# A gated long convolution and a token mixer: other order and other shapes for the loads of the first chunk

## The chip, the core and the metric

The kernel runs on one core of one Trainium2 chip. A core has TensorE (matrix products), VectorE, ScalarE and GpSimd (elementwise work), SyncE, which issues most of the transfers, and 16 DMA engines that carry them. The metric is the device time of one execution in microseconds (us), lower is better. The profile calls the engines PE (and PEld for its weight loads), DVE, ACT, POOL and SP; "SPq" and "ACTq" rows are DMA issues on SyncE's and ScalarE's queues.

## What is computed

One block on x = q, S = 2048 tokens by D = 640 channels, in 32-bit floats:

```python
mod = (silu(c) @ w_mod)                      # six rows of 640: sa, ca, ga, sb, cb, gb
h = layernorm(q) * (1 + ca) + sa
kv = short_conv(k, shift_k) * v              # 4 taps, causal, per channel
y = long_conv(kv, ssm_k) + kv * ssm_D        # causal, over all 2048 tokens, by FFT
x = q + ga * (h * y)
h = layernorm(x) * (1 + cb) + sb
out = x + gb * mlp_over_tokens(h)            # 2048 -> 1728 -> 2048, GELU, biases
```

## The kernel before

**Stages.** The first stage is the gated long convolution, in five chunks of 128 channels (loop at line 503); the second is the token mixer (from line 648). The convolution of a chunk is done by matrix products: `step1` (line 208, products of line 216) makes the first transform of kv (side 0) and of ssm_k (side 1), `f2` (line 222, products of line 232) the second transform together with the product of the two spectra, `i2` (line 253, products of line 261) and `i1` (line 268, products of line 277) the inverse. `gate` multiplies the result by the modulated layer norm A1 and adds it to q.

**How tokens lie.** A token is 32 m + 16 b + j. In the tiles of q, XH, partition 64 b + m holds the 16 rows j, so each half of the partitions belongs to one b. k, v, ssm_k and the taps are loaded by halves in the same way, h = 0 and 1 for 64 channels each (lines 127 to 153). Before, q comes in sixteen DMAs (lines 485 to 488): for every even j and each b one of 64 partitions with two neighbouring rows, that is 5,120 contiguous bytes a partition.

**What sets the order.** The schedule is written out by hand: every engine runs its instructions in the order of the program, and a DMA waits on the engine that issues it until the place that it writes is free; whatever stands behind it on that queue waits too. All transfers that matter here stand on SyncE's queue; ScalarE's queue has half of the first k and v, the first taps and the first ssm_D.

**Around the first chunk.** After the kv of chunks 0 and 1 (VectorE, with a share on GpSimd), SyncE issues the taps of chunk 2 (line 476), q, and the first four of five pieces of w_mod (line 494): piece kk is 128 rows of w_mod by the 1,920 columns of the first three modulation rows, one DMA each, cut into 2,560-byte runs. Piece 0 lies where ssm_k is loaded (T_aux), pieces 2 and 3 where the constant V1 of the inverse transform will lie (T_v1), piece 4 in P, which the spectra use until the end of f2.

Then, in chunk 0: VectorE takes the statistics of q (lines 526 to 529); TensorE does `step1(0, t)` for chunk 1, transposes the staged vectors (b1, b2 and c, in T_g), does i2(0), four of the five products with w_mod (`mod_part`, line 347), i2(1), the fifth product, the three rows that are spread over the partitions (`mod_row`, line 358), i1 for both halves, each followed by `gate`, and `step1(1, t)`, with which chunk 1 can start. SyncE issues ssm_k of chunk 1 when the first product has read piece 0 (`load_ks(1)`, line 546), V1 when the fourth has read piece 3 (line 547), and then k and v of chunk 2. ScalarE normalizes q (line 284) in sixteen operations of 128 x 128, in four portions; VectorE then applies the modulation rows (`po`).

Of the kernel before, what the change touches and what calls it, by code (L numbers as in the profile page):

```python
# [15 lines left out]
DC = 128  # L16
# [33 lines left out]
def mixer_kernel(ctx: ExitStack, tc: tile.TileContext, q, k, v, shift_k, ssm_k, ssm_D, w1, b1, w2, b2, c,  # L50
# [23 lines left out]
    def dram(t, offset, ap):  # L74
        return bass.AP(tensor=t.tensor, offset=t.offset + offset, ap=ap)
# [66 lines left out]
                           dram(k, 29 * D + DC * c + 64 * h, [[32 * D, 63], [D, 3], [1, 64]]))  # L142

    def load_taps(c, eng=sync):
        for h in range(2):
            eng.dma_start(TR[64 * h:64 * h + 64], dram(shift_k, (DC * c + 64 * h) * 4, [[0, 64], [1, 256]]))

    def load_ks(c, eng=sync):
        for h in range(2):
# [58 lines left out]
    def step1(side, t, later=False):  # L208

        ps = psum()  # L210
        for a in range(8):
            i = 8 * t + a
            lhs = KSP[:, i] if side else X.rearrange("p (m i) -> p i m", i=32)[:, i]
            o = 512 * (a % 2) + 128 * (a // 2)
            for ri in range(2):
                pe.matmul(ps[64 * ri:64 * ri + 64, o:o + 128], lhs, F1[:, 128 * ri:128 * ri + 128], start=True,  # L216
                          stop=True)
        evac = lambda: act.activation(Z[:, side, t].rearrange("p a k e -> p e a k"),  # L218
                                      ps.rearrange("p (e a k) -> p e a k", a=8, e=2), AF.Copy)
        return evac if later else evac()  # L220
# [60 lines left out]
    def a1_ops(c):  # L281

        g = lambda G: G[:, None, c * DC:(c + 1) * DC].to_broadcast([128, 16, DC])
        ac = [lambda j=j: act.activation(A1[:, j], XR(j, DC * c, DC), AF.Identity, scale=rs1[:, j:j + 1],
                                         bias=nm1[:, j:j + 1]) for j in range(16)]
        po = [lambda: TT(dve, A1, A1, g(G1), ALU.mult), lambda: TT(dve, A1, A1, g(G0), ALU.add)]
        if c == 0:
            def scaled(h):
                a, gh = A1[:, 8 * h:8 * h + 8], lambda G: G[:, None, 0:DC].to_broadcast([128, 8, DC])
                return [lambda: TT(dve, a, a, gh(G1), ALU.mult), lambda: TT(dve, a, a, gh(G0), ALU.add)]  # L290
            po = scaled(0) + scaled(1)
        return ac, po
# [46 lines left out]
    def mod_load(i, kk, place):  # L339
        sync.dma_start(place, dram(w_mod, 128 * kk * 6 * D + i * 640, [[6 * D, 128], [1, 1920]]),  # L340
                       max_dma_last_dim=2560)
# [140 lines left out]
    for t in range(4):  # L482
        step1(1, t)

    for j in range(0, 16, 2):
        for b in range(2):
            sync.dma_start(XH[j // 8][64 * b:64 * b + 64, j % 8:j % 8 + 2],
                           dram(q, (16 * b + j) * D, [[32 * D, 64], [D, 2], [1, D]]))

    three = lambda t: [t[:, 640 * j:640 * j + 640] for j in range(3)]  # L490
    pl = [three(t) for t in (T_aux, T_aux[:, 2048:3968], T_v1, T_v1[:, 1920:3840], P)]

    for kk in range(4):
        mod_load(0, kk, (T_aux[:, 0:1920], T_aux[:, 2048:3968], T_v1[:, 0:1920], T_v1[:, 1920:3840])[kk])

    fill = kv_ops(3)

# [5 lines left out]
    for c in range(NC):  # L503
        cn = c + 1 if c + 1 < NC else None
        ac, po = a1_ops(c)
        pend_m = pend_a = None
        for g in range(8):
            m_, a_ = f2(g)
            if pend_m:
                pend_m()  # L510
            if pend_a:
                pend_a()
            pend_a, pend_m = (pend_m and pa_next), m_
            pa_next = a_
            if c:
                for f_ in ac[2 * g:2 * g + 2]:
                    f_()
            dv(-(-len(fill) // max((6 if c else 8) - g, 1)))
            if c and cn is not None and g == 3:
                perm_add(cn)  # L520
        pend_m()
        if pend_a:
            pend_a()
        pa_next(dve if c else pool)
        if c == 0:
            for j in range(16):
                for h in range(2):
                    dve.bn_stats(bst[:, j, h, :], XR(j, 320 * h, 320))
                dve.bn_aggr(mv[:, j, :], bst[:, j, 0:2, :])
        if c and c + 2 < NC:  # L530
            taps()
            if c + 3 < NC:
                load_taps(c + 3)
        if c == 0:
            mod_load(0, 4, P[:, 0:1920])
            for t in range(4):
                step1(0, t)
            ps = psum()
            pe.transpose(ps[:, 0:36], stg, ID[0:36, 0:36])
            act.activation(cols, ps[:, 0:36], AF.Copy)  # L540
            act.activation(sil, cols[:, 30:35], AF.Silu)
            i2(0)
            for kk in range(4):
                mod_part(tap, kk, pl[kk])
                if kk == 0:
                    load_ks(1)
            sync.dma_start(T_v1[:, 0:4096], c_v1, max_dma_last_dim=4096)
            rstd(rs1, nm1, 0, 16)
            run(ac[0:4])
            i2(1)  # L550
            mod_part(tap, 4, pl[4])
            load_k(2, 1)
            load_k(2, 2)
            load_v(2, 2)
            load_halo(2)
            load_k(2, 0)
            load_v(2, 0)
            load_v(2, 1)
            load_k(2, 3)
            load_v(2, 3)  # L560
            mod_sum(tap, T_kt[:, 0:640])
            run(ac[4:8])
            pool.tensor_scalar(PW, TR.rearrange("p (i s) -> p s i", s=4), 1.0, None, op0=ALU.mult)
            run(kv_ops(2, pool))
            for i in range(3):
                mod_row(i, T_kt[:, 0:640])
            taps()
            load_taps(3)
            perm_add(1, dve)
            perm(1)  # L570
            load_ks(2)
            run(ac[8:16])
            run(po[0:2])
            fill.extend(kv(3, ((0,), (1, 2), (3,))))
        elif cn is not None:
            for t in range(2):
                step1(0, t)
            perm(cn)
            if c + 2 < NC:
                fill.extend(kv(c + 3 if c + 3 < NC else None))  # L580
            else:
                fill.extend(x1s(cc, j) for cc in range(c) for j in range(16))
        else:
            for kk in range(3, 5):
                mod_load(3, kk, pl[kk])
            T_wb = [mem("w0", 4096, "wb0"), mem("w1", 4096, "wb1")]
            split_w(0)
            run(po)
            for kk in range(3):
                mod_part(tap, kk, three(pl[kk]))  # L590
            load_w(1, T_aux[:, 0:2048])
            load_w(2, P)
            load_w(3, X)
        if c:
            dv(7 if cn is not None else 8)
            i2(0)
            if cn is None:
                split_w(1)
                split_w(2, mem("in", 4288, "wb2"))
            else:  # L600
                run(po)
                step1(0, 2)
            i2(1)
            if cn is not None:
                step1(0, 3)
                dv(3)
                if c + 2 == NC:
                    load_w(0)
        if cn is None:
            for kk in range(3, 5):  # L610
                mod_part(tap, kk, three(pl[kk]))
            split_w(3, mem("y", 4096, "wb3"))
            load_w(4)
            mod_sum(tap, T_t[:, 0:640])
        if c and cn is not None and c + 2 < NC:
            load_ks(c + 2)
        for half in range(2):
            ps = i1(half)
            if c and cn is None:
                dv(4)  # L620
            elif c and half:
                dv(3)
            elif c:
                k0 = step1(1, 0, True)
            elif half:
                run(po[2:4])
            if cn is not None:
                gate(c, ps, half)
            elif half == 0:
                gate(c, ps, 0, dve)  # L630
        if cn is not None:
            spill(c)
        if cn is not None:
            if c:
                k0()
            for t in range(1 if c else 0, 4):
                step1(1, t)
            if cn == NC - 1:
                dv(12)
                fill.extend(x1s(c, j) for j in range(16))  # L640
                pl = [T_in[:, 0:1920], T_in[:, 1920:3840], T_aux[:, 0:1920], T_z[:, 0:1920], T_z[:, 1920:3840]]
                for kk in range(3):
                    mod_load(3, kk, pl[kk])
            else:
                dv(11 if c else 8)
# [354 lines left out]
```

## Time and profile before

| | us |
|---|---|
| three timed runs: median | 741.24 |
| lowest, highest | 734.45, 748.2 |
| the profiled execution | 737.33 |
| its span, first to last instruction | 735.5 |
| TensorE busy in it | 653.1 |
| VectorE busy | 499.4 |
| ScalarE busy | 299.5 |
| GpSimd busy | 176.2 |

In the rows of an engine's instructions in order of time, the first number is the start in us from the span's start, the second the time taken, then engine, line, operation, tiles, shape and count; square brackets give idle time ahead of it and what ended it. A 32-bit product appears as more than one record. In rows that group instructions, the numbers behind the first bar are busy us and mean ns of one, those behind the second the idle time before them. In rows of windows each engine has busy us and number of instructions, then come the granted clock of TensorE, the mean busy share of the 16 DMA engines and the GB/s that they moved. Rows of waits have us in total, times, and the longest. The line 59 in a row is a helper through which elementwise operations are issued.

### The profile page before, as it was taken

How to read it: one execution, taken by the hardware profiler on the slowest of the kernel's cores; microseconds unless marked ns; L12 is line 12 of the kernel's file. 1: busy time of each engine (PE TensorE's matmuls, PEld its weight loads, DVE VectorE, ACT ScalarE, POOL GpSimd, SP SyncE). 2: the span in 40 equal slices, each digit the busy share in tenths (PEclk: the TensorE clock that was granted, in tenths of full speed). 3: DMA queues.
4: the chain of work that ended last, by engine and by line, in shares of the span. 5: the costliest groups of instructions: out<-in, count | busy, mean ns of one | idle time of the engine just before them, and what ended most of it. 6: DMA issues, size and time to landing. Idle time of an engine off the chain costs nothing.

```text
span 735.5 us, 20693 instructions
## 1 busy us (share of the span) xinstructions
PE 653.1 (89%) x9107; PEld 630.5 (86%) x9107; DVE 499.4 (68%) x857; ACT 299.5 (41%) x441; POOL 176.2 (24%) x176
## 2 busy tenths in 40 slices
PE   0797969999999989655899999999999989999997
PEld 0787749989989978544899999999999989999997
DVE  7756659969877548488994321231298958888886
ACT  0432465645646535425665512321235322333222
POOL 5197048626329047022440000000000000000000
PEclk9999889999999999657899999999999999999999
DMA  9989988445420174950000535335163333555410
GB/s 180 241 235 255 265 228 167 97 80 132 89 61 4 29 198 151 187 116 2 0 1 21 95 77 96 58 59 110 55 186 101 92 117 110 153 164 172 145 55 36
DMA packets 171921, 84.90 MB, mean 115 GB/s; under 512 B 88852, under 2 KB 165431, under 8 KB 171831
## 3 DMA queue, kind: packets, MB, share of 16 engines
q1 hardware_dynamic: 167282, 82.26, 45.5%
q10 hardware_dynamic: 4548, 1.31, 1.1%
q8 instruction: 71, 1.16, 0.7%
q14 instruction: 20, 0.16, 0.1%
HBM read 73.07 MB, written 10.49 MB: 114 GB/s over the span
## 4 chain that ended last, share of the span: by engine, by line
PE 58%; DVE 22%; issue 6%; DMA 4%; POOL 4%; ACT 3%; SPq 2%; ACTq 0%; DVEq 0%; POOLq 0%
PE pst L424 26%; PE pst L216 9%; PE pst L941 7%; PE pst L232 6%; DVE m_w L59 4%; PE pst L261 4%; POOL y L59 3%; PE pst L277 3%; DVE m_x L59 3%; DVE tap L59 3%; DVE kt L59 2%; ACT m_w L854 2%; PE pst L866 2%; DVE m_x L875 1%; DVE m_v L59 1%
## 5 line engine op out<-in xcount | busy, mean ns | idle before, releaser
L232 PE MATMUL pst<-z,w 128*64 128x64 f32 x2560 | 96.8, 241 | 11.7 <-ACT z L218 6.1
L232 PEld LDWEIGHTS pst<-z,w 128*64 128x64 f32 x2560 | 95.3, 142 | 13.6 <-ACT z L218 7.3
L424 PE MATMUL pst<-r_z,wb 128*128 128x320 f32 x504 | 82.9, 321 | 16.4 <-ACT r_z L685 11.3
L59 POOL TENSOR_TENSOR y<-p 128x256 f32<-128x256 f32 x72 | 90.4, 1304 | 26.8 <-DVE p L59 26.6
L424 PEld LDWEIGHTS pst<-r_z,wb 128*128 128x128 f32 x504 | 79.1, 198 | 18.3 <-ACT r_z L685 12.5
L59 DVE TENSOR_TENSOR p<-pst,kt 128x512 f32<-128x512 f32 x80 | 52.7, 690 | 28.5 <-ACT kt L236 19.3
L216 PE MATMUL pst<-v,x 128*64 128x128 f32 x640 | 46.0, 303 | 23.6 <-DVE x L59 23.6
L218 ACT ACTIVATE z<-pst 128x1024 f32<-128x1024 f32 x40 | 45.8, 1146 | 48.6 <-PE pst L216 28.4
L216 PEld LDWEIGHTS pst<-v,x 128*64 128x64 f32 x640 | 44.0, 221 | 24.2 <-POOL t L449 23.6
L424 PE MATMUL pst<-h_x,wb 128*128 128x320 f32 x336 | 51.1, 309 | 0.0
L424 PEld LDWEIGHTS pst<-h_x,wb 128*128 128x128 f32 x336 | 49.7, 188 | 0.0
L236 ACT ACTIVATE kt<-pst 128x512 f32<-128x512 f32 x40 | 25.2, 630 | 59.4 <-PE pst L232 38.8
L261 PEld LDWEIGHTS pst<-v,y 32*128 32x128 f32 x1280 | 42.6, 204 | 6.8 <-issue 2.6
L261 PE MATMUL pst<-v,y 32*128 32x64 f32 x1280 | 44.7, 291 | 4.2 <-DVE y L59 1.4
L746 ACT ACTIVATE pst<-pst,sm 128x640 f32<-128x640 f32 x14 | 10.7, 767 | 86.1 <-PE pst L424 86.1
L59 DVE TENSOR_TENSOR wb<-x,wb 128x1024 fp32r<-128x1024 f32 (+1 forms) x32 | 36.8, 1188 | 12.0 <-ACT wb L413 11.9
L866 PE MATMUL pst<-r_z,m_w 128*128 128x320 f32 x222 | 42.8, 312 | 1.9 <-DVE m_w L59 1.4
L216 PE MATMUL pst<-v,p 128*64 128x128 f32 x640 | 37.8, 274 | 2.4 <-issue 2.4
L854 ACT ACTIVATE m_w<-m_v 128x896 fp32r<-128x896 f32 x24 | 22.2, 950 | 42.4 <-DVE m_v L59 29.5
L424 PE MATMUL pst<-h_a,wb 128*128 128x320 f32 x252 | 38.8, 309 | 0.0
L424 PE MATMUL pst<-r_v,wb 128*128 128x320 f32 x252 | 38.8, 309 | 0.0
L216 PEld LDWEIGHTS pst<-v,p 128*64 128x64 f32 x640 | 35.2, 137 | 3.6 <-issue 3.2
(213 smaller groups left out, 1272.2 us busy)
## 6 DMA issues: line engine op xcount, KB each, us to landing
x<-in_B_w_dram SPq DMA_DIRECT2D x24, 512.0 KB
m_v<-in_B_w_dram SPq DMA_DIRECT2D x15, 384.0 KB
x<-in_B_w_dram SPq DMA_DIRECT2D x14, 384.0 KB
aux<-in_A_ssm_k_dram SPq DMA_DIRECT2D x10, 512.0 KB
in<-in_A_k_dram SPq DMA_DIRECT2D x36, 128.0 KB
in<-in_A_v_dram SPq DMA_DIRECT2D x36, 128.0 KB
m_x<-xs SPq DMA_DIRECT2D x28, 160.0 KB
out_dram<-m_x SPq DMA_DIRECT2D x28, 160.0 KB
```

The costliest lines, as they stand in the source:

```text
L59: TT = lambda eng, o, a, b, op: eng.tensor_tensor(o, a, b, op=op)
L216: pe.matmul(ps[64 * ri:64 * ri + 64, o:o + 128], lhs, F1[:, 128 * ri:128 * ri + 128], start=True, stop=True)
L218: evac = lambda: act.activation(Z[:, side, t].rearrange("p a k e -> p e a k"), ps.rearrange("p (e a k) -> p e a k", a=8, e=2), AF.Copy)
L232: pe.matmul(ps[64 * h:64 * h + 64, o:o + 64], W2[k1 // 32][:, 2 * (k1 % 32) + ri], rhs, start=True, stop=True)
L236: act.activation(kt.rearrange("p (m i) -> p m i", i=32), pv[:, :, 1], AF.Copy)
L261: pe.matmul(pp[qd // 2][:, o:o + 64], Y[p, ri, i:i + 2].rearrange("p i k -> p (i k)"), V2[p, 64 * ri:64 * ri + 64], start=ri == 0, stop=ri ...
L277: pe.matmul(ps[64 * b:64 * b + 64, 512 * e + 64 * jj:512 * e + 64 * jj + 64], V1[p, ri, n2], T2[p, :, 32 * ri + n2], start=ri == 0, stop=r ...
L424: pe.matmul(ps[0:m, h, 0:320], w_.bitcast(F32R), r_[:, 320 * h:320 * h + 320].bitcast(F32R), start=first and i == 0, stop=last and i == 2)
L746: act.activation(p, p, AF.Gelu_apprx_tanh, bias=B1C[:, f:f + 1])
L854: act.activation(W[n][0].bitcast(F32R), a(w_), AF.Copy)
L866: pe.matmul(bank[n], w[:, i].bitcast(F32R), r.bitcast(F32R), start=i == 0 and k == 0, stop=i == 6 and k == 2)
L941: pe.matmul(acc[s][:, h, 0:320], w[:, f_].bitcast(F32R), u[r + h].bitcast(F32R), start=f_ == 0 and k == 0, stop=f_ == NF - 1 and k == 2)
```

## The change

Everything concerns chunk 0 and the loads ahead of it.

- The taps of a chunk come in one DMA instead of two.
- ssm_k of chunk 1 is loaded ahead of q.
- q comes in sixteen DMAs of one row j each, for all 128 partitions; the source pattern is [[16 D, 2], [32 D, 64], [1, D]].
- Each piece of w_mod comes in three DMAs of 640 columns, at other places: pieces 0 and 1 in T_v1, 2 in T_aux, 3 in T_kt and T_t, 4 in G0, G1 and T_t. Three are issued behind q, two after the transpose.
- The transpose stands ahead of `step1(0, t)`, the five products behind it in a row, i2(0) and i2(1) after them. V1 is issued after the second product.
- The layer norm of q is done on VectorE in sixteen operations, ahead of the modulation rows. GpSimd's taps and its kv of chunk 2 stand behind the products in the program; ssm_k of chunk 2 is issued ahead of the taps of chunk 3.

```diff
-        for h in range(2):
-            eng.dma_start(TR[64 * h:64 * h + 64], dram(shift_k, (DC * c + 64 * h) * 4, [[0, 64], [1, 256]]))
+        eng.dma_start(TR, dram(shift_k, DC * c * 4, [[256, 2], [0, 64], [1, 256]]))
...
+            ac = [lambda j=j: dve.tensor_scalar(A1[:, j], XR(j, 0, DC), rs1[:, j:j + 1], nm1[:, j:j + 1], op0=ALU.mult,
+                                                op1=ALU.add) for j in range(16)]
...
-    for j in range(0, 16, 2):
-        for b in range(2):
-            sync.dma_start(XH[j // 8][64 * b:64 * b + 64, j % 8:j % 8 + 2],
-                           dram(q, (16 * b + j) * D, [[32 * D, 64], [D, 2], [1, D]]))
+    load_ks(1)
+    for j in range(16):
+        sync.dma_start(XR(j), dram(q, j * D, [[16 * D, 2], [32 * D, 64], [1, D]]))
...
-    pl = [three(t) for t in (T_aux, T_aux[:, 2048:3968], T_v1, T_v1[:, 1920:3840], P)]
-
-    for kk in range(4):
-        mod_load(0, kk, (T_aux[:, 0:1920], T_aux[:, 2048:3968], T_v1[:, 0:1920], T_v1[:, 1920:3840])[kk])
+    pl = [three(T_v1), three(T_v1[:, 1920:3840]), three(T_aux[:, 2048:3968]),
+          [T_kt[:, 0:640], T_kt[:, 640:1280], T_t[:, 640:1280]], [G0, G1, T_t[:, 0:640]]]
+
+    def load_piece(kk):
+        for j in range(3):
+            sync.dma_start(pl[kk][j], dram(w_mod, 128 * kk * 6 * D + 640 * j, [[6 * D, 128], [1, 640]]))
+
+    for kk in range(3):
+        load_piece(kk)
...
         if c == 0:
+            perm_add(1, dve)
             for j in range(16):
...
         if c == 0:
-            mod_load(0, 4, P[:, 0:1920])
-            for t in range(4):
-                step1(0, t)
             ps = psum()
             pe.transpose(ps[:, 0:36], stg, ID[0:36, 0:36])
             act.activation(cols, ps[:, 0:36], AF.Copy)
             act.activation(sil, cols[:, 30:35], AF.Silu)
-            i2(0)
-            for kk in range(4):
+            load_piece(3)
+            load_piece(4)
+            for t in range(4):
+                step1(0, t)
+            perm(1)
+            for kk in range(5):
                 mod_part(tap, kk, pl[kk])
-                if kk == 0:
-                    load_ks(1)
-            sync.dma_start(T_v1[:, 0:4096], c_v1, max_dma_last_dim=4096)
-            rstd(rs1, nm1, 0, 16)
-            run(ac[0:4])
-            i2(1)
-            mod_part(tap, 4, pl[4])
+                if kk == 1:
+                    sync.dma_start(T_v1[:, 0:4096], c_v1, max_dma_last_dim=4096)
...
+            load_ks(2)
             mod_sum(tap, T_kt[:, 0:640])
-            run(ac[4:8])
-            pool.tensor_scalar(PW, TR.rearrange("p (i s) -> p s i", s=4), 1.0, None, op0=ALU.mult)
-            run(kv_ops(2, pool))
+            rstd(rs1, nm1, 0, 16)
+            i2(0)
+            run(ac)
             for i in range(3):
                 mod_row(i, T_kt[:, 0:640])
             taps()
+            pool.tensor_scalar(PW, TR.rearrange("p (i s) -> p s i", s=4), 1.0, None, op0=ALU.mult)
             load_taps(3)
-            perm_add(1, dve)
-            perm(1)
-            load_ks(2)
-            run(ac[8:16])
+            run(kv_ops(2, pool))
+            i2(1)
             run(po[0:2])
```

## The prediction

> **What bounds the kernel now.** I read the page's head, then the busy time by windows around the first chunk, then TensorE, SyncE and ScalarE in order of time there, and last the DMA queues and issues. The profiled execution took 737.33 us, 1.8 us more than its span; the three timed runs have a median of 741.24.
>
> ```profile
> span 735.5 us, 20693 instructions
> ```
>
> The change lies between 44 us, when SyncE comes to the loads of q, and 116.5 us, when TensorE starts the first transform of chunk 1. TensorE in that stretch:
>
> ```profile
> 66.51 9.40 PE L216 MATMUL pst<-v,x 128*64 128x128 f32 x128
> ...
> 77.08 5.57 PE L261 MATMUL pst<-v,y 32*128 32x64 f32 x124 [0.62 <-ACT z L218]
> 82.57 3.84 PE L347 MATMUL tap<-aux,sm 128*32 128x320 f32 x24
> 86.24 2.32 PE L347 MATMUL tap<-v,sm 128*32 128x320 f32 x24
> 88.49 3.80 PE L261 MATMUL pst<-v,y 32*128 32x64 f32 x128
> 92.22 1.28 PE L347 MATMUL tap<-p,sm 128*32 128x320 f32 x12
> ...
> 99.95 3.54 PE L277 MATMUL pst<-z,v 64*64 64x64 f32 x142 [2.96 <-DMA v<-in_const_v_dram]
> 104.35 1.90 PE L277 MATMUL pst<-z,v 64*64 64x64 f32 x114 [0.86 <-issue]
> ```
> ```profile
> L216 PE MATMUL pst<-v,p 128*64 128x128 f32 x128 | 7.6, 274 | 1.5 <-issue 1.5
> ```
> ```profile
> 115.37 1.10 ACT L218 ACTIVATE z<-pst 128x1024 f32<-128x1024 f32 x1 [0.60 <-PE pst L216]
> ...
> 116.52 8.71 PE L232 MATMUL pst<-z,w 128*64 128x64 f32 x229 [1.19 <-ACT z L218]
> ```
>
> The reader sees TensorE nearly always at work: the modulation products and inverse transforms follow each other, with one 2.96 us wait for a constant. Beside it the transfers (DMA share and GB/s are the last columns, the granted clock is before them):
>
> ```profile
> core 0: us, PE busy (x) PEld busy (x) DVE busy (x) ACT busy (x) POOL busy (x), PEclk, DMA share, GB/s
> 49.00:70.00 21.00, 15.79 (x362) 15.48 (x360) 12.50 (x22) 4.25 (x7) 18.41 (x16) 0.92 1.03 234
> 72.00:82.00 10.00, 9.38 (x183) 8.94 (x182) 9.65 (x31) 4.59 (x6) 0.00 (x0) 0.84 1.04 395
> 86.00:92.00 6.00, 6.00 (x154) 4.42 (x152) 1.14 (x6) 1.65 (x4) 0.00 (x0) 1.00 1.11 177
> 78.90:85.70 6.80, 6.80 (x86) 4.70 (x85) 5.86 (x19) 3.38 (x5) 0.00 (x0) 0.51 0.66 250
> ```
>
> All 16 DMA engines are full in the first three. In the first they load q into 64 partitions at a time, 234 GB/s. In the second they load w_mod into 128 partitions, 395 GB/s, so 24.7 GB/s an engine. In the third ssm_k passes (1.05 MB in 6 us). The rate of q looks like the half-filled destination, and with 128 partitions q would need 5.24 MB / 395 = 13.3 us in place of 22.4. [...]
>
> **How many engines a DMA uses.** One row of the queues tells it. Queue q10 is ScalarE's, with these issues:
>
> ```profile
> q10 hardware_dynamic: 4548, 1.31, 1.1%
> ```
> ```profile
> in<-in_A_k_dram ACTq DMA_DIRECT2D x4, 128.0 KB
> in<-in_A_v_dram ACTq DMA_DIRECT2D x4, 128.0 KB
> ...
> rows<-in_A_shift_k_dram ACTq DMA_DIRECT2D x4, 64.0 KB
> ...
> rows<-in_A_ssm_D_dram ACTq DMA_DIRECT2D x2, 0.2 KB
> ```
>
> Data packets, one per contiguous run: 8 x 512 runs of 256 bytes (k, v), 4 x 64 of 1 KB, 2 x 1, together 4354. Of the 4548, 194 are left: 12 x 16 + 2 x 1. So each engine that takes part posts one packet more; the twelve patterns with 64 outermost ran on 16 engines, the two with 1 ran on one. The outermost count sets the number. The old q pattern has 64 outermost on both sides. The new one has 128 partitions in SBUF, but in DRAM [[16 D, 2], [32 D, 64], [1, D]]: outermost 2, and 16 D then 32 D can't be merged into one step. No row here has sides that differ. I take 2 engines, always the same two, as the nearest reading of "the outermost count sets it": a share for each engine has to be cut on both sides, and the DRAM side can be cut only in two.
>
> [...]
>
> **The change part by part, with its sum.** SyncE's queue:
>
> ```profile
> 45.81 0.49 SPq L146 DMA_DIRECT2D rows<-in_A_shift_k_dram  x1
> 46.34 5.07 SPq L487 DMA_DIRECT2D xa<-in_A_q_dram  x8
> 51.46 10.56 SPq L487 DMA_DIRECT2D xb<-in_A_q_dram  x8
> ...
> 84.98 3.25 SPq L150 DMA_DIRECT2D aux<-in_A_ssm_k_dram  x2
> 88.27 2.62 SPq L153 DMA_DIRECT2D rows<-in_A_ssm_D_dram  x2
> 91.48 0.39 SPq L547 DMA_DIRECT2D v<-in_const_v_dram  x1
> 91.93 0.62 SPq L130 DMA_DIRECT2D in<-in_A_k_dram  x1
> ```
> ```profile
> SPq L487 <- DMA xa<-in_A_q_dram: 6.4, 6, 2.2
> SPq L146 <- DMA w<-in_const_w_dram: 5.5, 1, 5.5
> ```
>
> 1. Taps by one DMA (outermost 2 in DRAM again: two engines, 64 KB each, 2.7 us at 24.7 GB/s, against 128 KB on 16). The first taps gate VectorE's start:
>
> ```profile
> 4.43 0.61 DVE L449 TENSOR_SCALAR tap<-rows 128x256 f32<-128x256 f32 x1 [2.75 <-DMA rows<-in_A_shift_k_dram]
> ...
> 6.08 0.70 DVE L59 TENSOR_TENSOR tap<-in,tap 128x512 f32<-128x512 f32 x1 [1.04 <-DMA in<-in_A_k_dram]
> ```
>
> Alone the taps would land 2.3 us later (2.7 against 0.3); the two engines share with k, so up to 4. 1.04 us of it hides behind the wait for k. Ends 0 and 4; I take 2.0, and all of chunk 0 shifts by it. On ScalarE's queue k stands behind them.
>
> 2. ssm_k(1) ahead of q. The wait rows show at most eight DMAs of SyncE in flight: q's first eight go out at once, the next wait for xa; the second taps DMA waits for the w constant, eight issues before it. With the taps in one, ssm_k(1) has that place and goes out at 45.8: 3.25 + 2.62 = 5.9 us of issue, in which the data pass too. q starts 5.9 us later: first issue 51.7, first packets about 1.4 us behind, with the taps' 2.0 at 55.1. What reads it early, two VectorE additions ahead of the statistics and ScalarE's copy, finds it landed. At 85 its place is free, so 5.9 us less stand ahead of the constant of L547.
>
> 3. q. Two engines carry 49.4 GB/s. A DMA of 320 KB takes 6.63 us, sixteen 106.1: the last row lands at 161.2. Waiting for it are VectorE's statistics, tile by tile, so only the last (two of the row below and an aggregate, about 1 us) is left at the end; nothing else is due on VectorE there. Queued behind it: every DMA of SyncE has a sixteenth on those two engines. So w_mod, 4.92 MB in fifteen DMAs of 320 KB, has 307 KB on each of them and needs 12.4 us more, wherever its other shares are: 173.6, about 1 us to tell.
>
> ```profile
> L528 DVE BATCH_NORM_STATS2 sm<-xa 128x6 f32<-128x320 f32 x16 | 6.7, 463 | 0.0
> ```
>
> The fourth and fifth piece go where the transform's buffers and the staged vectors lie; their readers, the last products of f2 and the transpose (now ahead of L216), are done by 76, so they wait for q alone.
>
> 4. Five products in a row, ahead of both inverse transforms: TensorE waits from about 78 us on. The last product, 1.28, ends at 175.9. From there by rows: L261 3.80; ScalarE's copies of it and of two rows, below, before the next buffers are free, 3.55; L261 3.80; copies 2.17; L277 twice at full clock, 3.80; L216 7.6 with 1.5 of stall; copy 1.10. Sum 27.3.
>
> ```profile
> 92.33 2.17 ACT L264 ACTIVATE z<-pst 128x512 f32<-128x512 f32 x4 [3.28 <-PE pst L261]
> ...
> 96.97 0.70 ACT L363 ACTIVATE g<-pst 128x640 f32<-128x640 f32 x1 [0.40 <-PE pst L358]
> 97.57 0.70 ACT L365 ACTIVATE g<-pst 128x640 f32<-128x640 f32 x1
> ```
>
> After a wait of 90 us the clock will be down: the windows show 0.51 for 6.8 us, which costs 3.4. Chunk 1 starts at 206.6 instead of 116.5.
>
> 5. LN(q) on VectorE: sixteen 128x128 operations, between the 0.18 us of its 128x16 and the 0.48 us of ScalarE's 128x128, 3 to 8 us:
>
> ```profile
> L312 DVE TENSOR_SCALAR sm<-sm 128x16 f32<-128x16 f32 x1 | 0.2, 179 | 0.0
> ```
> ```profile
> L284 ACT ACTIVATE aux<-xb,sm 128x128 f32<-128x128 f32 x8 | 3.2, 478 | 0.0
> ```
>
> They start about 167 (the statistics end at 162, eight small operations follow), while TensorE waits for w_mod, and cost nothing; were q fast they would run beside the inverse transforms. The constant for L277 is issued after the second product (about 169), 2.1 MB lands by 178 and is wanted at 189. k and v of chunk 2 go out from 169, 38 us ahead of chunk 1, where now it is 25 (116.5 - 91.9), which also covers GpSimd's part of kv, now behind the products: nothing. From chunk 1 on everything shifts as it is.
>
> Sum: 206.6 - 116.5 = +90.1, on 737.3: 827.4. Against the median, 3.9 above the profiled time, it would be 831; the range covers it.
>
> **Rivals.** (a) Sixteen engines all the same, because the DMA is cut otherwise than I read, or the pairs rotate over the eight DMAs in flight: q by 53.1 + 13.3 = 66.4, w_mod by 78.8 and told at 79.8. TensorE ends L216 at 76 and, after 5 x 1.28, the products at 82.5; with 27.3 and 3.4 chunk 1 starts at 113.2: 3.3 less, 734. For it: the two rates. Against: the q10 row. This is the other side, no slower; the point that decides is the number of engines: with w_mod told later than 84.5 it is a loss, q then taking 18 us, so some 12 engines. (b) The 234 GB/s come from the distance of q's rows, not from half a destination: 14.6 GB/s an engine, 11.2 us a DMA, 179.5 for q, 73.4 more: 901. No row separates the two; but 234 to 395, 0.59, lies near the half that half a destination suggests. (c) Sixteen engines at 234: q 22.4 us, w_mod told at 88.9, chunk 1 at 120.9: 742.
>
> **How the numbers follow.** Two engines 0.82; (a) 0.12; (b) 0.04; (c) 0.02. About 2% is what a measurement of this kernel can tell from no change. Two engines and (b) are slower by more, 0.86; (a) and (c) lie within 2%, 0.14, with 0.01 of it for faster. The range is that of the likeliest case: down 19 for an engine at 26 GB/s (-7), no cold clock (-3), no shift by the taps (-2) and (-7) for waits of TensorE that fall away; up 19 for a second cold stretch (3), taps (2), gaps between q's DMAs (3) and the runs' scatter, whose highest lies 10.9 over the profiled one. 808 to 846 holds nearly all of the 0.82.
>
> **What would show it.** Right: q1's packets fall short of a sixteenfold posting; a stretch of 100 us with the DMA share near 0.13 and 50 GB/s; TensorE idle from about 78 to 162; SyncE's issues of the later q 6.6 us apart; the waiters on L528 named as DMA xa and xb. Wrong: a share of 1.0 and 395 GB/s from 53 to 79, and products that end near 82; then (a) holds, and the 827 falls with it.

## The result and the profile after

| | median of the runs, us | lowest to highest |
|---|---|---|
| before | 741.01 | 734.45 to 748.2 |
| after | 838.83 | 834.37 to 842.55 |

Before has a fourth run here, of 740.79. The ratio of after to before is 1.1351, with a 95% interval of 1.1249 to 1.1453: the change makes the kernel slower by 13.5%. The profiled execution of after took 837.62 us with a span of 835.8, 100.3 more than before.

The page of after, the rows of transfers by fortieths of the span and of the two queues:

```profile
DMA  8871111487336432065840005434344333444430
GB/s 150 219 177 50 50 50 50 138 270 144 92 77 121 91 53 55 3 152 187 156 102 2 1 1 101 87 66 80 73 95 134 105 109 113 148 140 126 140 123 33
...
q1 hardware_dynamic: 168152, 82.26, 38.8%
q10 hardware_dynamic: 4488, 1.31, 0.9%
```

Four slices in a row, 84 us, have 50 GB/s. The packets say why. Queue q1 had 167,282 of them before. One row a run instead of two gives 1,024 more for q, ten more DMAs of w_mod 160 more. If q's sixteen DMAs post 2 packets each beyond their data instead of 16, that is 224 fewer; three taps of 2 instead of six of 16 are 90 fewer. The sum is 168,152, to the packet; with sixteen engines throughout it would be 168,418. On q10 the taps leave 4 such packets of 64, which is the 60 that are missing there.

The same stretch by windows (columns as before: engines, granted clock, DMA share, GB/s):

```profile
100.00:150.00 50.00, 0.00 (x0) 0.00 (x0) 8.77 (x24) 0.00 (x0) 0.00 (x0) 0.50 0.13 50
```

0.13 of sixteen engines is two engines, full. TensorE does nothing for 50 us, and VectorE only what each arriving tile of q gives it. TensorE's one wait, 92.71 us for w_mod, stands in its rows further down; VectorE waits for each tile of q:

```profile
DVE sm L535 <- DMA xb<-in_A_q_dram: 45.7, 8, 6.7
DVE sm L535 <- DMA xa<-in_A_q_dram: 36.0, 7, 5.4
```

SyncE's queue in order of time. Its issue of q alone takes 91 us: the median issue takes 6.4 us, about as long as one of these DMAs runs, and for these issues no wait for a DMA in flight is recorded, so why the issue itself is held is not shown:

```profile
46.99 0.59 SPq L145 DMA_DIRECT2D rows<-in_A_shift_k_dram  x1
53.36 4.37 SPq L149 DMA_DIRECT2D aux<-in_A_ssm_k_dram  x2
57.78 2.71 SPq L152 DMA_DIRECT2D rows<-in_A_ssm_D_dram  x2
60.53 38.43 SPq L489 DMA_DIRECT2D xa<-in_A_q_dram  x8
99.01 52.36 SPq L489 DMA_DIRECT2D xb<-in_A_q_dram  x8
151.41 12.17 SPq L497 DMA_DIRECT2D v<-in_w_mod_dram  x6
```

VectorE's statistics, which follow the arrival of q, and its layer norm:

```profile
142.16 0.89 DVE L535 BATCH_NORM_STATS2 sm<-xb 128x6 f32<-128x320 f32 x2 [5.42 <-DMA xb<-in_A_q_dram]
...
148.72 0.89 DVE L535 BATCH_NORM_STATS2 sm<-xb 128x6 f32<-128x320 f32 x2 [5.42 <-DMA xb<-in_A_q_dram]
...
162.85 0.89 DVE L535 BATCH_NORM_STATS2 sm<-xb 128x6 f32<-128x320 f32 x2 [6.44 <-DMA xb<-in_A_q_dram]
...
170.72 0.89 DVE L535 BATCH_NORM_STATS2 sm<-xb 128x6 f32<-128x320 f32 x2 [6.74 <-DMA xb<-in_A_q_dram]
...
186.38 0.25 DVE L316 RECIPROCAL sm<-sm 128x16 f32<-128x16 f32 x1 [14.31 <-ACT sm L315]
...
187.78 2.14 DVE L287 TENSOR_SCALAR aux<-xa,sm 128x128 f32<-128x128 f32 x8
189.84 4.18 DVE L287 TENSOR_SCALAR aux<-xb,sm 128x128 f32<-128x128 f32 x8
```

Tiles come 6.56 us apart: 327,680 bytes in 6.56 us is 50.0 GB/s. TensorE behind that:

```profile
171.53 4.99 PE L349 MATMUL tap<-v,sm 128*32 128x320 f32 x23 [92.71 <-DMA v<-in_w_mod_dram]
...
184.01 3.80 PE L260 MATMUL pst<-v,y 32*128 32x64 f32 x128
...
192.32 7.08 PE L260 MATMUL pst<-v,y 32*128 32x64 f32 x124
201.25 6.13 PE L276 MATMUL pst<-z,v 64*64 64x64 f32 x256 [1.85 <-ACT z L263]
...
217.38 7.82 PE L231 MATMUL pst<-z,w 128*64 128x64 f32 x206 [1.23 <-ACT z L217]
```

Chunk 1 starts at 217.38, where before it started at 116.52: 100.9 later, and the whole span is 100.3 longer. So, in these two profiled executions, all of the loss arises ahead of chunk 1.

### The profile page after: what moved, and what is told of

The parts are those of the page before. It is cut to its first block, busy times and chain, and to the rows that moved or that the text cites. A ratio compares the mean times of both kernels' runs of the same rounds, so it can differ in the third digit from the quotient of the medians.

```text
span 835.8 us, 20696 instructions
## 1 busy us (share of the span) xinstructions
PE 664.4 (79%) x9107; PEld 637.2 (76%) x9107; DVE 510.7 (61%) x873; ACT 293.2 (35%) x425; POOL 177.0 (21%) x176
## 3 DMA queue, kind: packets, MB, share of 16 engines
q1 hardware_dynamic: 168152, 82.26, 38.8%
## 4 chain that ended last, share of the span: by engine, by line
PE 45%; DVE 20%; SPq 16%; DMA 7%; issue 4%; POOL 4%; ACT 3%; ACTq 0%; DVEq 0%; POOLq 0%
PE pst L426 23%; SPq L489 11%; PE pst L944 6%; PE pst L260 4%; PE pst L215 4%; DVE m_w L59 4%; POOL y L59 3%; PE pst L276 3%; PE pst L231 3%; DVE tap L59 3%; DVE m_x L59 2%; DVE kt L59 2%; DMA aux<-in_w_mod_dram 2%; ACT m_w L857 1%; PE pst L869 1%
## 5 line engine op out<-in xcount | busy, mean ns | idle before, releaser
L349 PE MATMUL tap<-v,sm 128*32 128x320 f32 x24 | 5.2, 596 | 92.7 <-DMA v<-in_w_mod_dram 92.7
L349 PEld LDWEIGHTS tap<-v,sm 128*32 128x32 f32 x24 | 1.8, 134 | 95.8 <-DMA v<-in_w_mod_dram 95.1
L215 PE MATMUL pst<-v,x 128*64 128x128 f32 x640 | 47.9, 314 | 28.9 <-DVE x L59 28.9
L215 PEld LDWEIGHTS pst<-v,x 128*64 128x64 f32 x640 | 45.9, 221 | 29.6 <-issue 26.4
L260 PEld LDWEIGHTS pst<-v,y 32*128 32x128 f32 x1280 | 45.6, 216 | 6.5 <-issue 2.3
L260 PE MATMUL pst<-v,y 32*128 32x64 f32 x1280 | 48.0, 303 | 3.1 <-DVE y L59 1.6
L749 ACT ACTIVATE pst<-pst,sm 128x640 f32<-128x640 f32 x14 | 10.7, 766 | 86.1 <-PE pst L426 86.1
```

Source lines behind the costliest of these rows:

```text
L260: pe.matmul(pp[qd // 2][:, o:o + 64], Y[p, ri, i:i + 2].rearrange("p i k -> p (i k)"), V2[p, 64 * ri:64 * ri + 64], start=ri == 0, stop=ri ...
L749: act.activation(p, p, AF.Gelu_apprx_tanh, bias=B1C[:, f:f + 1])
```

## The experiments

**1. The change with q, the taps, or both loaded by halves again; and the kernel before with nothing but the new q load.** These four share one set of runs of the kernel before (median 740.12). The three from the kernel after differ by these lines:

```diff
-            sync.dma_start(XR(j), dram(q, j * D, [[16 * D, 2], [32 * D, 64], [1, D]]))
+        for b in range(2):
+            sync.dma_start(XR(j)[64 * b:64 * b + 64], dram(q, (16 * b + j) * D, [[32 * D, 64], [1, D]]))
...
-        eng.dma_start(TR, dram(shift_k, DC * c * 4, [[256, 2], [0, 64], [1, 256]]))
+        for h in range(2):
+            eng.dma_start(TR[64 * h:64 * h + 64], dram(shift_k, (DC * c + 64 * h) * 4, [[0, 64], [1, 256]]))
```

The first edit alone is `q_halves`, the second alone `taps_halves`, both `both_halves`. What was expected of them, in this order:

> The changed kernel, but q comes by halves: two DMAs for each row j, each for 64 partitions with 64 outermost in DRAM. Taps stay in one DMA. Theory (two engines for a source pattern with 2 outermost): q takes 22.4 us (the 234 GB/s of 64 partitions) in place of 105, starts where it starts in the changed kernel (issue at 60.5), w_mod follows 12.4 us later, chunk 1 starts near 132 instead of 217: about 753 us. Rival (the loss lies in the new order: ssm_k ahead of q, five products ahead of the inverse transforms): stays within 15 us of 838.

> The changed kernel with the taps by two DMAs of 64 partitions again, q on two engines still. The prediction priced the taps in one DMA at 2.0 us (ends 0 and 4): 837. The trace of the changed kernel has ssm_k(1) issued 7.5 us later than in the kernel before, and SyncE's first k loads held for 4.4 us by the taps: if all of that is the taps, 831.

> The changed kernel with both q and the taps by halves: what is left is the order (ssm_k first, products in a row, layer norm on VectorE, w_mod in fifteen DMAs). Theory: sixteen engines at 234 GB/s, case (c) of the prediction, 742 us, that is no difference to the kernel before within 1%. Rival (the order costs of its own): over 750.

The kernel before with the new load, `q_rows_alone`:

```diff
-    for j in range(0, 16, 2):
-        for b in range(2):
-            sync.dma_start(XH[j // 8][64 * b:64 * b + 64, j % 8:j % 8 + 2],
-                           dram(q, (16 * b + j) * D, [[32 * D, 64], [D, 2], [1, D]]))
+    for j in range(16):
+        sync.dma_start(XR(j), dram(q, j * D, [[16 * D, 2], [32 * D, 64], [1, D]]))
```

> The kernel before with one part of the change alone: q by sixteen DMAs of whole rows for 128 partitions, source pattern with 2 outermost. Theory: q takes 105 us from 47.7, w_mod's shares on the two engines 12.4 us more, and since the inverse transform and ssm_k stand in the old order around the products, chunk 1 starts near 190: about 811 us (800 to 825). Rival (the order makes the loss): within 15 us of 741.

| | median, us | ratio to before, 95% interval |
|---|---|---|
| q_halves | 753.32 | 1.0163, 1.0097 to 1.023 |
| taps_halves | 832.56 | 1.1236, 1.116 to 1.1312 |
| both_halves | 746.46 | 1.0084, 1.0048 to 1.0121 |
| q_rows_alone | 827.83 | 1.1153, 1.1059 to 1.1248 |

From `taps_halves` to `both_halves` only q's pattern changes: 86.1 us. From `q_halves` to `both_halves` only the taps': 6.9 us, against the 2.0 of the prediction. What is left, 6.3 us, is everything else together: the order, w_mod in fifteen DMAs at other places, the layer norm on VectorE, and q in 32 DMAs of one row where before has 16 of two. The three add up to 99.3, and after lies 97.8 above before in the runs of the result. The load does it alone too: put into the old order it costs 87.7 us. `q_halves` came out as expected, `taps_halves` near its 831; `both_halves` lies between its two expectations of 742 and over 750, so the rest does cost something, but less than the rival had.

`q_rows_alone` came out 17 us above its expectation and outside the 800 to 825 given with it. In its trace q's last tile reaches VectorE at 158.01, w_mod is still waited for at 169.87, and the second inverse transform behind it takes 7.11 us, where before has 3.80:

```profile
162.70 11.04 SPq L150 DMA_DIRECT2D aux<-in_A_ssm_k_dram  x2
```
```profile
169.87 1.93 PE L347 MATMUL tap<-v,sm 128*32 128x320 f32 x12 [3.05 <-DMA v<-in_w_mod_dram]
171.72 7.11 PE L261 MATMUL pst<-v,y 32*128 32x64 f32 x128
...
185.59 4.11 PE L277 MATMUL pst<-z,v 64*64 64x64 f32 x142 [1.14 <-DMA v<-in_const_v_dram]
...
202.77 14.38 PE L232 MATMUL pst<-z,w 128*64 128x64 f32 x384 [1.20 <-ACT z L218]
```

Chunk 1 starts at 202.77, 13 us later than the 190 expected. From chunk 3 to chunk 4 another 7.6 us are lost (58.8 for 51.2), in a stretch that the edit does not touch; the second inverse transform of chunk 3 takes 7.11 us there, in before 3.96. The issue of ssm_k took 11.04 us instead of 3.25 and held V1 back until 177.01, but TensorE waited only 1.14 us for V1. Nor is the pair of engines shown to be what slowed this issue: it took 7.42 us in `ks_behind` and 12.24 in `v1_early`, where q and the taps come by halves.

That `both_halves` still loses is seen on TensorE:

```profile
78.70 6.24 PE L350 MATMUL tap<-v,sm 128*32 128x320 f32 x23 [7.63 <-DMA v<-in_w_mod_dram]
...
100.03 7.46 PE L261 MATMUL pst<-v,y 32*128 32x64 f32 x121
...
124.97 14.36 PE L232 MATMUL pst<-z,w 128*64 128x64 f32 x384 [1.24 <-ACT z L218]
```

The five products stand ahead of both inverse transforms, so TensorE has nothing beside the load: a wait of 7.63 us, and the second inverse transform takes 7.46 us, with a granted clock of 0.50 from 100 to 108. Chunk 1 starts 8.5 us later than before.

**2. The outermost count of the source, 4, 8 and 128.** The taps are by halves, the destination is all 128 partitions as in the change, only the source pattern differs. These kernels load other tokens of q than the computation needs; the bytes are the same.

```diff
-        sync.dma_start(XR(j), dram(q, j * D, [[16 * D, 2], [32 * D, 64], [1, D]]))
+        sync.dma_start(XR(j), dram(q, j * D, [[4 * D, 4], [63 * D, 32], [1, D]]))      # q_outer4
+        sync.dma_start(XR(j), dram(q, j * D, [[2 * D, 8], [126 * D, 16], [1, D]]))     # q_outer8
+        sync.dma_start(XR(j), dram(q, j * D, [[16 * D, 128], [1, D]]))                 # q_outer128
+        sync.dma_start(XR(j), dram(q, j * D, [[3 * D, 8], [16 * D, 16], [1, D]]))      # q_outer8_near
```

> The changed kernel with the taps by halves and q by sixteen DMAs for 128 partitions whose source pattern has 4 outermost and 32 below it. It loads other tokens of q than it should, so the output differs; bytes, runs of 2,560 bytes and destination are as in the change. Theory (the outermost count of the source is the number of engines): q takes 53 us instead of 105 (2 outermost) and 22.4 (halves), so against the 746.5 with halves 30 more: 777 us. Rival (any source pattern that cannot be merged falls to two engines, or the interleaved destination halves are the trouble): about 832. Rival (the distance of the rows in DRAM sets the rate, here 161 KB): over 832.

> The same with 8 outermost and 16 below it, distance of the inner rows 322 KB; other tokens again. Theory: eight engines, q in 26.5 us, 4 more than with halves: 750 us. Rivals: about 832, or more by the distance.

> The same with one outermost count of 128 (row 16 p + j to partition p; other tokens than it should, distance 41 KB). Theory: sixteen engines and all partitions, 395 GB/s as w_mod, q in 13.3 us, 9 less than with halves: 737 us, the prediction's case (a) had 734. Rival (q's rate is set by the distance of its rows, not by the half destination): 746, as with halves.

> The changed kernel with taps by halves and q by sixteen DMAs for 128 partitions with 8 outermost and 16 below it as in q_outer8, but with near rows: 3 rows and 16 rows apart (41 KB) in place of 2 and 126 (322 KB). Other tokens than it should. q_outer8 took 759.6 where 24.7 GB/s an engine would give 750; its q ran at 145 to 150 GB/s, 18.5 an engine. If the distance of the rows did that, this one gives 750; if it is the number of engines or the places that they write, 759 again.

The window from 57 to 68 us, while q is loaded, in `q_outer4`:

```profile
57.00:68.00 11.00, 9.67 (x196) 9.50 (x193) 9.66 (x19) 5.22 (x7) 10.44 (x10) 1.00 0.27 104
```

in `q_outer8`:

```profile
57.00:68.00 11.00, 8.89 (x177) 8.72 (x174) 9.55 (x19) 4.98 (x7) 10.61 (x10) 1.00 0.54 149
```

in `q_outer128`:

```profile
57.00:68.00 11.00, 9.38 (x189) 9.22 (x187) 9.47 (x12) 5.14 (x7) 10.49 (x10) 1.00 1.02 380
```

and in `q_outer8_near`:

```profile
57.00:68.00 11.00, 9.36 (x199) 9.19 (x196) 9.62 (x11) 4.81 (x8) 11.00 (x10) 1.00 0.53 145
```

The last two columns are the answer. The share is 0.13, 0.27, 0.54 and 1.02 for an outermost 2, 4, 8 and 128: that many engines of sixteen, and sixteen at 128. Times: `q_outer4` 778.61 (ratio 1.0555, 1.0504 to 1.0606), as expected; `q_outer8` 759.59 (1.0287, 1.0232 to 1.0343), 9 above; `q_outer128` 739.5 (1.0023, 0.9993 to 1.0053). `q_outer128` lies nearer the 737 of its theory than the 746 of the rival. Two, four and sixteen engines moved 50, 104 and 380 GB/s, about 25 each. Eight engines, though all busy (share 0.54), moved 149 GB/s, 18.6 each. The 9 us follow from it: 5.24 MB at 149 take 35 us, 13 more than by halves. `q_outer8_near`, with the rows 41 KB apart instead of 323, moves 145 in the profiled execution, which speaks against the distance as the reason. Its times do not decide: the four runs scatter from 750.43 to 768.69 (median 762.68, the profiled one 763.48), and the lowest is what the distance would have given.

**3. The halves from two queues.** The old pieces of q, those of b = 0 from SyncE and those of b = 1 from ScalarE, to have both halves of the partitions filled at the same time.

```diff
-    for j in range(16):
-        sync.dma_start(XR(j), dram(q, j * D, [[16 * D, 2], [32 * D, 64], [1, D]]))
+    for j in range(0, 16, 2):
+        for b in range(2):
+            both[b].dma_start(XH[j // 8][64 * b:64 * b + 64, j % 8:j % 8 + 2],
+                              dram(q, (16 * b + j) * D, [[32 * D, 64], [D, 2], [1, D]]))
```

> The changed kernel with the taps by halves and q in the old pieces (two neighbouring rows for 64 partitions), the lower half of the partitions on SyncE's queue and the upper on ScalarE's, so that both halves are filled at once. Right output. If half a destination is what holds q to 234 GB/s, both queues together give near 395: q in 13.3 us, w_mod told near 80, about 737 us. If the rate belongs to the rows' distance or to the pattern, 746. ScalarE spends 8 x 0.6 us on the issues ahead of its first copies for f2, which may give back up to 3.

It took 754.26 (1.022, 1.0187 to 1.0252) instead of 737. Nothing held ScalarE's half back, so it was issued from 40.5 on, 31 us ahead of SyncE's (71.4). In the window of 44 to 56 us

```profile
44.00:56.00 12.00, 5.00 (x136) 4.84 (x132) 0.00 (x0) 1.08 (x2) 3.10 (x3) 0.84 1.07 200
```

all engines were full at 200 GB/s in all, most of it this half, with some loads of k and v beside it, and a load of k, wanted at 40, came at 59.9. The wait:

```profile
DVE tap L59 <- DMA in<-in_A_k_dram: 19.9, 1, 19.9
```

SyncE's half, issued from 71.43 to 77.89 and with only w_mod behind it, shows nearly the same rate:

```profile
72.00:84.00 12.00, 11.67 (x215) 11.32 (x211) 10.89 (x26) 6.36 (x8) 8.57 (x8) 1.00 0.95 195
```

The halves were never filled together, so the question put was not answered. What it gives is that one half alone was filled at 195 to 200 GB/s.

**4. Three orders that might win back the 6.3 us.** From `both_halves`: `ks_behind` issues ssm_k(1) behind the last piece of w_mod again; `i2_first` also puts both inverse transforms ahead of the products; `v1_early` starts from `i2_first`.

```diff
# ks_behind, from both_halves
-    load_ks(1)                 # ahead of q
-            perm_add(1, dve)
...
             load_piece(4)
+            load_ks(1)
-            perm(1)
-            load_ks(2)
...
+            perm_add(1, dve)
+            perm(1)
+            load_ks(2)         # behind kv_ops(2, pool)
# i2_first, besides
+            i2(0)
+            i2(1)
             for kk in range(5):
                 mod_part(tap, kk, pl[kk])
...
-            i2(0)
...
-            i2(1)
# v1_early, from i2_first
-            load_ks(1)
...
             i2(0)
-            i2(1)
-            for kk in range(5):
+            for kk in range(3):
                 mod_part(tap, kk, pl[kk])
                 if kk == 1:
                     sync.dma_start(T_v1[:, 0:4096], c_v1, max_dma_last_dim=4096)
+            load_ks(1)
+            rstd(rs1, nm1, 0, 16)
+            run(ac)
+            i2(1)
+            for kk in range(3, 5):
+                mod_part(tap, kk, pl[kk])
...
-            rstd(rs1, nm1, 0, 16)
-            run(ac)
```

> The changed kernel with q and taps by halves, and ssm_k(1) behind the last piece of w_mod instead of ahead of q (its reader on VectorE and ScalarE's copy behind the modulation rows again, ssm_k(2) behind them). Right output. What is left over the kernel before in both_halves is 6.3 us. Theory: q now starts about 6 us later than it could, because 16,384 short runs of ssm_k stand ahead of it, and w_mod with it, on which TensorE waits: 740 us, the difference to the kernel before gone. Rival (ssm_k ahead of q is hidden; the rest is the products' order): 746 as both_halves.

> ks_behind, and both inverse transforms i2(0), i2(1) ahead of the five products, where TensorE waits for w_mod. Right output. Theory: TensorE idles about 7 us ahead of the products because w_mod is behind q; two transforms of 3.8 us fit into it, and with them the copies between them leave the path: 734 us, faster than the kernel before by 1%. Rival (VectorE's chain of statistics, layer norm and modulation is the next bound at once): 739 to 740.

> i2_first with the first three products between the two inverse transforms, the V1 constant issued behind the second of them and ahead of ssm_k(1), and the statistics' tail and LN(q) ahead of the second inverse transform. Theory (i2_first gains nothing because V1, in the place of two pieces of w_mod, is issued late and lands at 101.7): V1 is issued near 82 instead of 92.8 and lands near 91, TensorE's wait of 9.0 us for it falls to 2 or less, and chunk 1 starts 6 to 8 us earlier than in i2_first (118.2): 734, about 4 under the kernel before. Rival (VectorE's chain of LN, gates and sums sets the end): V1 lands early, but VectorE's product of the first i1 still ends near 106 and chunk 1 starts within 2 us of 118: 740.

| | median, us | before, run beside it | ratio, 95% interval |
|---|---|---|---|
| ks_behind | 743.49 | 737.97 | 1.0065, 1.0032 to 1.0098 |
| i2_first | 741.17 | 737.97 | 1.0028, 1.0 to 1.0057 |
| v1_early | 740.12 | 739.43 | 1.0006, 0.9973 to 1.0039 |

None gains on the kernel before; `ks_behind` lies between its two expectations (ssm_k of a chunk is 8,192 runs of 128 bytes by its access pattern, not the 16,384 named there), and `i2_first` came out at its rival's time. In `i2_first` TensorE no longer waits for w_mod, but for V1, which is loaded into the place of the first two pieces:

```profile
101.80 6.88 PE L277 MATMUL pst<-z,v 64*64 64x64 f32 x256 [8.97 <-DMA v<-in_const_v_dram]
```

In `v1_early` (the profiled execution took 745.28) V1 lands 8.8 us earlier:

```profile
93.00 5.51 PE L277 MATMUL pst<-z,v 64*64 64x64 f32 x256 [1.78 <-DMA v<-in_const_v_dram]
...
108.27 6.37 PE L216 MATMUL pst<-v,p 128*64 128x128 f32 x64 [3.69 <-DVE aux L59]
115.83 14.37 PE L232 MATMUL pst<-z,w 128*64 128x64 f32 x384 [1.20 <-ACT z L218]
```

and chunk 1 starts at 115.83, 2.4 us ahead of `i2_first`, only 0.7 ahead of before. VectorE holds it now:

```profile
97.91 0.26 DVE L59 TENSOR_TENSOR aux<-aux,rows 1x64 f32<-1x64 f32 x1 [4.40 <-DMA rows<-in_A_ssm_D_dram]
...
106.98 1.23 DVE L59 TENSOR_TENSOR aux<-pst,aux 128x1024 f32<-128x1024 f32 x1
```

It waits for ssm_D(1), which now stands behind V1 and ssm_k(1) on SyncE's queue, and its last product with i1 ends at 108.2, where in `i2_first` it ended at 111.5. So the rival was right in the time, and in the mechanism with an addition: the chain on VectorE sets the end, and a new wait at its head takes most of what the early V1 gave.

## Why the prediction was right

The time of 838.83 lies 11 us above the sum of 827.4, within the range of 808 to 846, and the cause is the one forecast: two engines. By its steps, in the profiled execution, 10.8 us of start of chunk 1 were missing (100.9 against 90.1):

- **Step 1, the taps: right in direction, far too small.** Forecast 2.0 with an upper end of 4; the issue of ssm_k slipped from the forecast base of 45.8 to 53.36, 7.5 us, and `q_halves` against `both_halves` gives 6.9. The step counted one wait, VectorE's at the start; that is there, 2.85 us (7.28 in the row below, 4.43 before). What it left out is SyncE's queue behind the taps: its first four loads of k are issued in 7.83 us instead of 2.74, of which 4.4 is a wait for the taps, and every load behind them goes out later. These taps stand on ScalarE's queue; that the eight places in flight are common to both queues would explain the wait, but no row shows it. At the taps of chunk 2 the queue is 7.2 us late (46.99, 39.81 before). The sum shifted chunk 0 by VectorE's wait alone and did not apply its own limit of eight in flight here. After, VectorE's first row, SyncE's, and the wait in it:

```profile
7.28 0.61 DVE L451 TENSOR_SCALAR tap<-rows 128x256 f32<-128x256 f32 x1 [5.61 <-DMA rows<-in_A_shift_k_dram]
```
```profile
1.53 7.83 SPq L130 DMA_DIRECT2D in<-in_A_k_dram  x4
```
```profile
SPq L130 <- DMA rows<-in_A_shift_k_dram: 4.4, 1, 4.4
```

- **Step 2, ssm_k ahead of q: right.** 7.1 us of issue (4.37 + 2.71) for the forecast 5.9. With step 1, q's first issue is at 60.53 instead of 53.7: 6.8 of the 10.8.
- **Step 3, two engines: right.** 6.56 us a DMA for 6.63. That the DRAM side's count decides where the sides differ was the author's reading of a row with equal sides; the runs bear it out: beside 128 partitions as destination the load ran at 50, 104 and 380 GB/s, with DMA shares of 0.13, 0.27 and 1.02, for an outermost 2, 4 and 128. That every DMA goes to the same two engines no row shows. Only the end was off by 2.7: q's last two DMAs took 7.6 and 7.9, with the first w_mod loads issued from 151.41 on. The prediction had added w_mod's shares behind q; that a part of them came in between on q's two engines is the author's reading of this and of the products, which ended 13.4 after q's last row, not 14.7.
- **Step 4, five products in a row: right, 2.6 short, and partly by luck.** From the end of the products (184.07) to chunk 1 33.3 us passed, 30.7 were forecast: 27.3 of work and 3.4 for a low clock after the long wait. The 3.4 came from a window of before, at 0.51, in which TensorE was busy for all 6.80 us; that row shows no low clock after a wait. After has one, 0.50 behind the wait of 92.71 us (row below), but ahead of 184, where the last products still wait for w_mod, so nothing shows that it cost time:

```profile
171.50:174.00 2.50, 2.47 (x10) 0.96 (x12) 0.49 (x3) 0.00 (x0) 0.00 (x0) 0.50 0.92 285
```

  What counts is a second stretch of low clock (0.50 from 192 to 200, 0.65 from 200 to 208), which the range had with 3 us and the sum had not: the second inverse transform takes 7.08, where the first takes 3.80, and i1 6.13 for the 3.80 of the forecast, together 5.6. So the 3.4 stood in for a cost that it was not meant for.
- **Step 5, layer norm on VectorE: right in price, wrong in place.** 2.14 + 4.18 = 6.3 us, between 3 and 8. It does not start about 167 but at 187.78: the square root that it needs stands on ScalarE behind the copy of the five products' sums (0.70 us from 184.11), hence the 14.31 us in the row of L316. It stayed hidden because VectorE's next product waits for i1 anyway (5.09 us of idle time ahead of it, at 205.0). That is no more than the 5.6 us by which the half clock delayed i1, so at full clock, by this estimate, hardly any of the slack would have been left.

The rivals: (a), sixteen engines, and (c) fall by the share of 0.13. (b), that the distance of q's rows held it to 234 GB/s, falls by the same rows: at the same distance of 82 KB an engine of the change moves 25 GB/s, and by halves 14.6. What remains between 234 and 380 as the likely reason is that half of the partitions are filled; no run changes that alone, since `q_outer128` also halves the distance of the rows. The 195 to 200 GB/s for one half alone in `q_two_queues` and the 395 of w_mod into 128 partitions in before fit it.

Rival (a) can be read from `q_outer128`, the one with all sixteen engines and all partitions: 739.5, no different from before, where (a) had 734. q is there sooner, but the five products are spread over 12.8 us by the arrival of w_mod, and the second inverse transform takes 7.32 us, with a granted clock of 0.50 from 92 to 98. Its rows on TensorE:

```profile
71.37 5.39 PE L350 MATMUL tap<-v,sm 128*32 128x320 f32 x24 [0.50 <-DMA v<-in_w_mod_dram]
...
84.13 3.80 PE L261 MATMUL pst<-v,y 32*128 32x64 f32 x128
...
92.05 7.32 PE L261 MATMUL pst<-v,y 32*128 32x64 f32 x124
...
117.48 7.74 PE L232 MATMUL pst<-z,w 128*64 128x64 f32 x204 [1.23 <-ACT z L218]
```

From the first inverse transform to chunk 1 it takes 33.4 us, as in after, and chunk 1 starts at 117.48 for 116.52 before. So the new order of TensorE's work, with the half clock in it, gives back what a faster q would bring; how much of this is the order is not separated, as `q_rows_alone` has such a slow transform in the old order too.

## What to carry to other kernels

Read the outermost count of a DMA's source before merging two loads into one: here a destination of 128 partitions and the same bytes came at an eighth of the rate because the source began with a 2 (50 GB/s against 380 to 395). Count the packets that a queue has beyond its data; the one row of q10 before the change, with 194 of them, led to the two engines. And price a slower small transfer by what stands behind it, not by the wait that it ends: the taps cost 6.9 us here, and the wait at the start grew by 2.85.

## What the runs showed that was not expected

- Eight engines, with 16 rows each and 128 partitions as destination, moved 145 to 149 GB/s, 18 to 19 an engine, in one profiled execution at each of two row distances; two moved 25 an engine and four 26 (50 and 104 GB/s). Why is open.
- The granted clock fell although TensorE was busy. In after, with the inverse transforms and the row-spreading products one upon another:

```profile
184.00:188.00 4.00, 4.00 (x131) 3.91 (x131) 1.36 (x7) 2.36 (x4) 0.00 (x0) 1.00 1.18 283
188.00:192.00 4.00, 4.00 (x16) 2.59 (x14) 4.00 (x15) 3.01 (x6) 0.77 (x1) 0.56 0.56 117
192.00:200.00 8.00, 7.40 (x125) 6.90 (x124) 7.85 (x6) 1.73 (x4) 7.69 (x6) 0.50 0.75 168
```

TensorE is marked busy for 15.4 of these 16 us, and gets 1.00, then 0.56, then 0.50. These products take 32 partitions in, or one, instead of 128. In `v1_early`, where products of 128 partitions stand between the two inverse transforms, the second takes 3.80, at 1.00 from 76 to 92; in `both_halves` it took 7.46 (0.50 from 100 to 108), in `i2_first`, with one right behind the other, 6.64 (0.56 from 76 to 84). That the narrow products themselves let the clock fall is the author's reading of these rows; no run isolates it, and it is not the whole: in chunk 3, where products of 128 partitions stand on both sides and the program is the same, the transform took 3.96 us in before, at a granted clock of 1.00, and 7.11 us in `q_rows_alone`:

```profile
247.59 3.96 PE L261 MATMUL pst<-v,y 32*128 32x64 f32 x128
```
```profile
336.14 7.11 PE L261 MATMUL pst<-v,y 32*128 32x64 f32 x128
```

What separates these two stays open.
- One half of the partitions filled from one queue ahead of everything else took all sixteen engines (share 1.07) at about 200 GB/s in `q_two_queues`, and VectorE waited 19.9 us for a load of k.
